# A fused attention and feed-forward kernel: the first two token blocks with eight plain products in place of Strassen's seven, all elementwise sums on VectorE, and six staging buffers for the weights

## The chip, the cores and the metric

One core of a Trainium2 chip runs the kernel. The metric is device time in microseconds (us) of one execution; lower is better. The kernel before took 928.1 us, the median of three runs (927.41 to 931.62). The engines are TensorE (PE, with PEld for its weight loads), VectorE (DVE), ScalarE (ACT), GpSimd (POOL) and SyncE (SP, which here only issues DMAs). An engine works through its own instructions in order, and waits where one of them needs something that is not there yet.

## The reference

Inputs are q, k, v of shape (8 batches, 8 heads, 576 positions, 64) in float32, and w_in (512 x 2048) and w_out (2048 x 512), which arrive in float64.

```python
q_s = softmax(q, axis=-1)            # over the 64 features
k_s = softmax(k, axis=2)             # over the 576 positions
kv  = einsum('bhsd,bhse->bhde', k_s, v)
x   = einsum('bhsd,bhde->bhse', q_s, kv)   # then as 4608 tokens x 512
h   = x @ w_in
out = (h * sigmoid(1.702 * h)) @ w_out     # 4608 x 512
```

## The kernel before, in words

The 4608 tokens are nine blocks of 512. For a block, eight steps run; a step takes one pair of 128-wide column groups of w_in (group p and group p + 8), computes h for them (FFN1), applies the GELU, and adds the product with the matching 256 rows of w_out into four PSUM banks (FFN2). Odd blocks take the pairs backwards. Each float32 operand of these matmuls is held as a high part and a low part, and a product is three matmuls: high by high, high by low, low by high.

FFN1 uses Strassen's scheme in Winograd's form: w_in's pair (512 x 256) and the block's x (512 x 512) are taken as 2 x 2 quarters, and seven products of quarters (`ffn1`, line 714) replace eight. A product is six matmuls of 256 columns. Sums of quarters of x are made per block (`x_sums`, line 664, split into high and low at lines 681 and 684); sums of quarters of the weights are made once, in block 0, when a pair is first converted (`conv_wi`, lines 332 and 338). After a product, ACT copies a bank (line 738) and DVE adds banks together (line 727).

The float64 weights are converted to float32 by bit operations on their words: ACT takes the high word (`high`, line 288), DVE shifts and merges the low word (`low`, line 297, and `narrow`, line 293), ACT rounds the result to its high part, and a subtraction gives the low part (line 338 for w_in, 384 for w_out). The raw words of a pair's w_in and later of its w_out lie in the same tile (tags `wo{p}0` and `wo{p}1`), so w_out can only be loaded after w_in was merged. Converted w_in tiles `wa` and `wb` are a ring of two pairs; each pair is stored to DRAM in block 0 (line 341, on SP) and fetched again in later blocks by DMAs that GpSimd issues (line 360). w_out stays in SBUF.

Attention for the next block runs in between: maxima of k over positions (`k_max`), subtraction and exponential (`k_sub`), the k-by-v product (`kv_pairs`, line 562), softmax of q (`q_soft`), transposes, and the product that gives x (`x_pairs`, line 638). For batches 0 and 1 the maximum over partitions is made with a transpose on TensorE (lines 502 to 510), later with GpSimd's `partition_all_reduce` (line 488).

What sets the order: the function adds every operation to a `Plan` with an engine, a cost, what it reads and writes, and a rank. `due` gives each a due time, counted back from TensorE's operations in order of rank; `forward` then walks through time and lets each free engine take the ready operation that is due first. What comes out is the order in which each engine gets its instructions. Operations marked `EITHER` may go to DVE or POOL, whichever is free first; in blocks 0 and 1 these are the sums, subtractions and low parts. The plan books 0.5 us on SP for a DMA.

Of the kernel before, what the change touches and what calls it, by code (L numbers as in the profile page):

```python
# [18 lines left out]
class Plan:  # L19
# [7 lines left out]

# [3 lines left out]
    EITHER = ("DVE", "POOL")  # L31
# [22 lines left out]
    def due(self):  # L54
        ops = self.ops
        at = [float("inf")] * len(ops)
        time = 0.0
        for n in sorted((n for n, o in enumerate(ops) if o[0] == "PE"), key=lambda n: (ops[n][3], n)):
            at[n] = time
            time += ops[n][1]  # L60
        for n in reversed(range(len(ops))):
            for d in ops[n][2]:
                e, cost, _, _, _, _, size = ops[d]
                cost = cost[0] if e is self.EITHER else cost
                need = cost + self.HOP + (size / self.RATE + self.LAND if size else 0.0)
                at[d] = min(at[d], at[n] - need)
        return at

    def forward(self, due):
# [3 lines left out]
        ready = {e: [] for e in (*free, self.EITHER)}  # L73
# [5 lines left out]
        wire, table = 0.0, {"POOL": "sum"}  # L79
        began, start, end = [], [0.0] * len(ops), 0.0  # L80
        self.taken = {}
        now = 0.0
        while len(began) < len(ops):
# [3 lines left out]
            for e in free:  # L87
                mine = [ready[e]] + ([ready[self.EITHER]] if e in self.EITHER else [])
                mine = [r for r in mine if r]
                if free[e] > now or not mine:  # L90
                    continue
                _, n = heapq.heappop(min(mine))
                kind, cost, _, _, _, needs, size = ops[n]
                if kind is self.EITHER:
                    self.taken[n] = e
                    cost, needs = (cost[0], None) if e == "DVE" else (cost[1], needs)
# [17 lines left out]
            times = [f for e, f in free.items() if f > now and (ready[e] or e in self.EITHER and ready[self.EITHER])]  # L114
# [14 lines left out]
    def emit(self):  # L129
        for n in self.order():  # L130
            run = self.ops[n][4]
            if n in self.taken:
                run(self.taken[n])
            else:
                run()


def dve(n):
    return 0.16 + n / 920
# [4 lines left out]


def pool(n):
    return 0.25 + n / 440
# [3 lines left out]
def efficient_attention_then_gelu_ffn(  # L151
# [8 lines left out]
):  # L160

# [45 lines left out]
    engines = {"DVE": nc.vector, "POOL": nc.gpsimd}  # L207
    summed = []

    def sums():  # L210

        summed.append(("sums", len(summed)))
        return summed[-1]

    def sb_op(shared, n, reads, writes, rank, run):

        if shared:
            plan.add(
                plan.EITHER, (dve(n), pool(n)), reads, (*writes, sums()), rank, lambda e: run(engines[e]), table="sum"
            )  # L220
        else:
            plan.add("DVE", dve(n), reads, writes, rank, lambda: run(nc.vector))

    ident = sb("ident", [P, P])
    kvn = [sb(f"kvn{i}", [P, NP, D]) for i in range(2)]
    xa = sb("xa", [P, 2, 2, HT])
    xb = sb("xb", [P, 2, 2, HT])
    s1, s2, s4 = (sb(f"s{i}", [P, 2, HT]) for i in (1, 2, 4))
    xs = [[sb(f"x{s}{o}", [P, 2, HT], F32R) for s in "hl"] for o in range(7)]
    gt = [[sb(f"g{i}{u}", [P, 2, HT]) for i in range(2 - u)] for u in range(2)]  # L230
    gs = [[[sb(f"g{s}{i}{u}", [P, 2, HT], F32R) for u in range(2)] for i in range(2)] for s in "hl"]
    ta, ts, tu = (sb(f"t{s}", [P, HT]) for s in "asu")
# [7 lines left out]
    cols = [sb(f"col{i}", [P, 1]) for i in range(2)]  # L240
# [3 lines left out]
    wa = [sb(f"wa{i}", [P, 2, 3, 2 * P], F32R) for i in range(2)]  # L244
    wb = [sb(f"wb{i}", [P, 2, 4, 2 * P], F32R) for i in range(2)]
    kept = [
        (dram.tile([P, 2 * 3 * 2 * P], F32, name=f"ka{p}"), dram.tile([P, 2 * 4 * 2 * P], F32, name=f"kb{p}"))
        for p in range(NS)
    ]

    make_identity(nc, ident)
# [5 lines left out]
    plan.add("POOL", 0.7, (), ("ident",), -3000, lambda: None)  # L257
# [8 lines left out]
    def load_w(p, kind, rank):  # L266
        for jj in range(2):
# [11 lines left out]

            held = [("st", 1, jj, m) for m in range(3 + jj)] if p == SPARE and kind == "wi" else []  # L280
            plan.add("SP", plan.ISSUE, (), (tag, *held), rank + 0.01 * jj, run, size=2 * DM * 4 * P)
# [19 lines left out]

    stages = [None, None]
    SPARE = NS - 1

    def stage(p):
        n = p % 2 if p < SPARE else 0
        if stages[n] is None:
            stages[n] = [  # L310
                sb(f"st{n}{i}", [P, 3 + i, 2 * P], tag=f"wo{SPARE}{i}" if n else None) for i in range(2)
            ]
        return stages[n], [[("st", n, i, m) for m in range(3 + i)] for i in range(2)]

    def conv_wi(p, rank):
        i = p % 2
        (sa, sb_), (KA, KB) = stage(p)
        for jj, (s, K) in enumerate(((sa[:, 0:2], KA[0:2]), (sb_[:, 2:4], KB[2:4]))):
            T = f"wo{p}{jj}"
            f = flat(s)  # L320
# [3 lines left out]

            plan.add("ACT", 0.67, (T,), K, rank, lambda f=f, w=w: high(f, w()))
            plan.add("DVE", 0.40, (T,), (T,), rank, lambda w=w: low(w()))
            plan.add("DVE", 0.69, (T, *K), K, rank, lambda f=f, w=w: narrow(f, w()))
        B11, B21, T2, T1, T4, T3, B22 = [(sa[:, m], KA[m]) for m in range(3)] + [(sb_[:, m], KB[m]) for m in range(4)]
        for (o, ok), (x, xk), (y, yk) in ((T1, T3, B11), (T2, B22, T1), (T4, B21, T2), (T3, B22, T3)):

            def run(E, o=o, x=x, y=y):
                E.tensor_tensor(out=o, in0=x, in1=y, op=ALU.subtract)  # L332

            sb_op(True, 2 * P, (xk, yk), (ok,), rank, run)
        for u, tl, f, K, n in (("wa", wa[i], sa, KA, 3), ("wb", wb[i], sb_, KB, 4)):

            def run_l(E, tl=tl, f=f):
                E.tensor_tensor(out=tl[:, 1], in0=f, in1=tl[:, 0].bitcast(F32), op=ALU.subtract)  # L338

            def run_s(tl=tl, u=u):  # L340
                nc.sync.dma_start(out=kept[p][u == "wb"], in_=tl.bitcast(F32).rearrange("p s n f -> p (s n f)"))

            plan.add("ACT", act(n * 2 * P), K, ((u, i),), rank, lambda tl=tl, f=f: nc.scalar.copy(tl[:, 0], f))
            sb_op(True, n * 2 * P, (*K, (u, i)), ((u, i),), rank, run_l)
            plan.add("SP", plan.ISSUE, ((u, i),), ((u, "kept", p),), rank, run_s, size=n * 4 * P * P * 4)
# [6 lines left out]
    def load_kept(t, step):  # L352
# [4 lines left out]
        for u, tl, n, off in (("wa", wa[i], 3, 5), ("wb", wb[i], 4, 13)):  # L357

            def run(u=u, tl=tl):
                nc.gpsimd.dma_start(out=tl.rearrange("p s n f -> p (s n f)"), in_=kept[p][u == "wb"])  # L360

            plan.add("POOL", 1.0, ((u, "kept", p),), ((u, i),), R(t, step - 2, off), run, size=n * 4 * P * P * 4)

    nt = [0]

    def next_tmp():
        nt[0] += 1
        return nt[0] % 2

    def conv_wo(p, rank):  # L370
        for jj in range(2):
            i = next_tmp()
# [389 lines left out]
    def ffn2(t, step):  # L762
# [3 lines left out]
        for c in (2, 3, 0, 1):  # L766
# [15 lines left out]
            if step < NS - 1:  # L782
                continue
# [90 lines left out]
```

## Time and profile before

| what | value |
|---|---|
| median of three runs | 928.1 us |
| the profiled execution | 929.58 us |
| its span, first to last instruction | 927.7 us |
| mean granted TensorE clock | 0.971 |
| PE busy | 865.3 us (93%) |
| DVE busy | 557.3 us (60%) |
| ACT busy | 492.8 us (53%) |
| POOL busy | 180.7 us (19%) |

All times of single instructions and stretches come from this one execution. Of its 929.58 us, 1.9 us lie outside the span. An engine is busy from an instruction's start to its end, so an instruction that is held up while it runs counts as busy too. Where instructions of one engine follow each other closely, they overlap a little; what one costs is then the distance between two starts.

### The profile page before, as it was taken

Reading aid. Unit: us, or ns where it says so; the run is one execution under the profiler, and the core shown is the slowest. Engines: PE = TensorE matmul, PEld = TensorE weight load, DVE = VectorE, ACT = ScalarE, POOL = GpSimd, SP = SyncE. Lnnn points to the kernel's source line nnn. Section 1 sums busy time; section 2 is a strip of 40 time slices with the busy share of each in tenths; the row PEclk is TensorE's granted clock in tenths of the full one; section 3 lists DMA queues with packets and bytes.
Section 4 is the critical chain, followed back from the end, with each engine's and each line's share of the span. In section 5 each row is a group of like instructions: output and inputs, shape, how many; then the busy total and the mean of one; then the engine's idle time right before and its main releaser. Section 6 shows DMA issues by size and latency. Waiting matters only on the chain.

```text
span 927.7 us, 15134 instructions
## 1 busy us (share of the span) xinstructions
PE 865.3 (93%) x5896; PEld 750.5 (81%) x5896; DVE 557.3 (60%) x1080; ACT 492.8 (53%) x867; POOL 180.7 (19%) x204
## 2 busy tenths in 40 slices
PE   3678777899999999999999899999999999999998
PEld 2466656788888789889888798888988988898896
DVE  6899998977653558763535387644436643353333
ACT  3657765676853397863433777633347543343222
POOL 4665565732001201000002010010000000000100
PEclk9889877999999999999999999999999999999999
DMA  9956975359516866455167664542455255416541
GB/s 286 279 190 232 295 216 203 113 204 253 161 42 205 232 189 171 159 174 167 46 195 227 172 191 141 177 159 81 157 176 169 67 159 165 153 46 205 165 153 46
DMA packets 115272, 158.29 MB, mean 171 GB/s; under 512 B 75776, under 2 KB 94208, under 8 KB 108032
## 3 DMA queue, kind: packets, MB, share of 16 engines
q0 software_dynamic: 13824, 88.09, 29.6%
q1 hardware_dynamic: 101376, 69.22, 25.4%
q8 instruction: 47, 0.77, 0.3%
q14 instruction: 25, 0.20, 0.1%
HBM read 133.17 MB, written 24.12 MB: 170 GB/s over the span
## 4 chain that ended last, share of the span: by engine, by line
PE 76%; DVE 14%; DMA 4%; SPq 2%; issue 2%; ACT 2%; DVEq 0%; POOL 0%
PE bank L776 37%; PE bank L714 33%; PE bank L562 3%; DMA kt<-in_k 2%; PE bank L638 2%; PE bank L617 1%; DVE tmp L293 1%; DVE mx L483 1%; DVE raw L297 1%; DVE m L482 1%; DVE g L727 1%; DMA qt<-in_q 1%; DVE xl L684 1%; DVE st L332 1%; DVE w L384 1%
## 5 line engine op out<-in xcount | busy, mean ns | idle before, releaser
L776 PE MATMUL bank<-w,gh 128*128 128x512 f32 x1152 | 371.0, 403 | 3.8 <-DVE w L384 3.2
L714 PE MATMUL bank<-xh,wb 128*128 128x256 f32 x1152 | 254.4, 285 | 8.1 <-DVE ts L727 3.7
L776 PE MATMUL bank<-w,gl 128*128 128x512 f32 x576 | 231.0, 401 | 2.4 <-DVE gl L758 1.4
L714 PEld LDWEIGHTS bank<-xh,wb 128*128 128x128 f32 x1152 | 199.0, 192 | 24.3 <-DVE ts L727 4.6
L776 PEld LDWEIGHTS bank<-w,gh 128*128 128x128 f32 x1152 | 190.8, 191 | 25.2 <-DVE w L384 4.4
L714 PE MATMUL bank<-xh,wa 128*128 128x256 f32 x864 | 187.5, 291 | 15.3 <-DVE wa L338 6.6
L714 PEld LDWEIGHTS bank<-xh,wa 128*128 128x128 f32 x864 | 148.2, 195 | 28.8 <-DVE wa L338 7.4
L730 ACT ACTIVATE g<-g 128x512 f32<-128x512 f32 (+1 forms) x144 | 75.6, 525 | 171.3 <-DVE g L727 167.3
L714 PE MATMUL bank<-xl,wb 128*128 128x256 f32 x576 | 164.1, 285 | 0.3 <-DVE xl L684 0.3
L776 PEld LDWEIGHTS bank<-w,gl 128*128 128x128 f32 x576 | 109.8, 191 | 30.8 <-DVE gl L758 3.2
L714 PE MATMUL bank<-xl,wa 128*128 128x256 f32 x432 | 124.5, 288 | 2.0 <-POOL xl L684 2.0
L714 PEld LDWEIGHTS bank<-xl,wb 128*128 128x128 f32 x576 | 109.5, 190 | 11.8 <-DVE xl L684 0.5
L758 DVE TENSOR_TENSOR gl<-g,gh 128x512 fp32r<-128x512 f32 x136 | 93.5, 693 | 22.8 <-ACT gh L755 22.3
L727 DVE TENSOR_TENSOR tu<-bank,ta 128x256 f32<-128x256 f32 x72 | 30.3, 421 | 107.0 <-PE bank L714 106.8
L755 ACT CAST gh<-g 128x512 fp32r<-128x512 f32 x144 | 89.4, 621 | 4.3
L714 PEld LDWEIGHTS bank<-xl,wa 128*128 128x128 f32 x432 | 84.0, 195 | 7.7 <-POOL xl L684 2.3
L360 POOL DMA_DIRECT2D wa<-ka x48 | 25.9, 539 | 329.0 <-PE bank L714 329.0
L360 POOL DMA_DIRECT2D wb<-kb x48 | 25.5, 531 | 252.3 <-PE bank L714 250.9
L730 ACT ACTIVATE g<-bank 128x256 f32<-128x256 f32 x72 | 27.7, 385 | 78.7 <-PE bank L714 77.5
L738 ACT COPY ta<-bank 128x256 f32<-128x256 f32 x72 | 26.8, 372 | 59.8 <-PE bank L714 59.3
L727 DVE TENSOR_TENSOR g<-bank,ts 128x256 f32<-128x256 f32 x72 | 30.3, 421 | 40.6 <-PE bank L714 40.2
L727 DVE TENSOR_TENSOR g<-bank,tu 128x256 f32<-128x256 f32 x72 | 30.4, 422 | 37.1 <-PE bank L714 36.4
(103 smaller groups left out, 988.7 us busy)
## 6 DMA issues: line engine op xcount, KB each, us to landing
wb<-kb POOLq DMA_DIRECT2D x48, 1024.0 KB, 5.4
wa<-ka POOLq DMA_DIRECT2D x48, 768.0 KB, 4.8
out<-tmp SPq DMA_DIRECT2D x36, 256.0 KB, 3.1
kt<-in_k SPq DMA_DIRECT2D x32, 256.0 KB, 3.7
raw<-in_moe_w_in SPq DMA_DIRECT2D x16, 512.0 KB, 6.7
raw<-in_moe_w_out SPq DMA_DIRECT2D x16, 512.0 KB, 4.0
kb<-wb SPq DMA_DIRECT2D x8, 1024.0 KB, 5.2
vt<-in_v SPq DMA_DIRECT2D x56, 128.0 KB, 5.2
```

The source lines that it names most:

```text
L293: nc.vector.scalar_tensor_tensor(fi, fi, 3, w[:, :, 0], ALU.logical_shift_left, ALU.bitwise_or)
L297: nc.vector.tensor_scalar(lo, lo, 29, None, ALU.logical_shift_right)
L360: nc.gpsimd.dma_start(out=tl.rearrange("p s n f -> p (s n f)"), in_=kept[p][u == "wb"])
L562: nc.tensor.matmul(pk[r0 : r0 + D, m, cols], lhs, rhs, start=c == 0, stop=c == CM, tile_position=(0, r0))
L638: nc.tensor.matmul(po[ro], kvn[b % 2][ri, hp, :], qx[ri], start=True, stop=True, tile_position=((a ^ odd) * D, a * D),)
L714: nc.tensor.matmul(ph[bk], tl[:, s, place, c * P : (c + 1) * P], x[:, c, :], start=opens and c == 0 and e == 0, stop=c == 1 and e == 2, sk ...
L727: return lambda: nc.vector.tensor_tensor(out=o, in0=ph[bk], in1=x, op=ALU.add)
L730: return lambda: nc.scalar.activation(o, x, AF.Gelu_apprx_sigmoid)
L738: vec("ACT", act(n), (ZB,), (A,), 2, lambda: nc.scalar.copy(a, ph[Z]))
L755: vec("ACT", act(2 * n), half, (H,), slot, lambda c=c, gh=gh: nc.scalar.copy(gh, c))
L758: E.tensor_tensor(out=gl, in0=c, in1=gh.bitcast(F32), op=ALU.subtract)
L776: nc.tensor.matmul(bank[c], l, r, start=first_ and e == 0, stop=last and e == 2)
```

## The change

Blocks 0 and 1 compute FFN1 with eight plain products per step: two column groups times four quarters of 128 rows, each three matmuls of 512 columns (`plain1`). Block 0 therefore needs only w_in itself in high and low parts (`wj`), and `conv` converts w_in and w_out in the same way; staging uses two `tmp` tiles and four `wide` ones. Block 0 stores w_in's parts to DRAM; block 1 fetches them, and `sums` makes Strassen's four sums of w_in (`wt`) from them on DVE and stores those too. From block 2 on a step fetches three pieces in place of two, of 1 MB, 0.5 MB and 0.25 MB. Nothing is marked `EITHER` any more. The maximum over partitions is made by `partition_all_reduce` for all batches, and the identity matrix is built after batch 0's maxima.

```diff
-    EITHER = ("DVE", "POOL")
...
+    def conv(p, kind, rank):
+        for jj in range(2):
+            ff, T = next_tmp(6)
...
+            plan.add("ACT", 0.66, (K,), (T,), rank, lambda ff=ff, w=w: high(ff, w()))
+            plan.add("DVE", 0.38, (K,), (K,), rank, lambda w=w: low(w()))
+            plan.add("DVE", 0.69, (K, T), (T,), rank, lambda ff=ff, w=w: narrow(ff, w()))
+            plan.add("ACT", 0.62, (T,), (KD,), rank, c5)
+            plan.add("DVE", 0.69, (KD, T), (KD,), rank, c6)
...
+    def plain1(t, step):
+        i, gi = pair(t, step) % 2, step % 2
+        for jj, bk in enumerate((Y, Z)):
...
+                for e, (l, r) in enumerate(((0, 0), (0, 1), (1, 0))):
+                    nc.tensor.matmul(
+                        bank[bk], w[:, l, c, :], x[:, r], start=c == 0 and e == 0, stop=c == KC - 1 and e == 2
+                    )
...
-        if b > 1:
-            plan.add("POOL", 0.92, (M, *summed), (M,), rank, reduce, table="max")
-            return
+        plan.add("POOL", 0.92, (M,), (M,), rank, reduce, table="max")
...
-        sb_op(t < 2, e, (K, M), (K,), rank, run_b)
+        plan.add("DVE", 2 * dve(e), (K,), (K, M), rank, run_m)
...
-            at(R(t, p), lambda rank, t=t, p=p: ffn1(t, p))
+            at(R(t, step), lambda rank, t=t, step=step: (plain1 if t < 2 else ffn1)(t, step))
```

On SP, the kernel before has these rows between the sixth load of w_in and the first stores of converted tiles (`kt`, `vt`, `kl`, `vl` and `qt` are attention's tiles of batch 1, `ka` the DRAM copy):

```order
L273 DMA raw<-in_moe_w_in 128x4x256 x6
L448 DMA vt_113<-in_v 128x4x64 x2
L448 DMA vt_114<-in_v 128x4x64 x2
L448 DMA vt_115<-in_v 128x4x64 x2
L417 DMA kt_109<-in_k 128x2x256
L417 DMA kt_110<-in_k 128x2x256
L278 DMA raw<-in_moe_w_out 128x1024
L407 DMA kl<-in_k 64x8x64
L417 DMA kt_111<-in_k 128x2x256
L417 DMA kt_112<-in_k 128x2x256
L448 DMA vt_116<-in_v 128x4x64 x2
L278 DMA raw<-in_moe_w_out 128x1024 x3
```

The changed kernel has there, from the third of its four pairs of `vt` loads on (`kept` is the DRAM copy):

```order
L449 DMA vt_90<-in_v 128x4x64 x2
L449 DMA vt_91<-in_v 128x4x64 x2
L469 DMA qt_92<-in_q 16x8x64
L469 DMA qt_92<-in_q 112x8x64
L408 DMA kl<-in_k 64x8x64
L418 DMA kt_86<-in_k 128x2x256
L418 DMA kt_87<-in_k 128x2x256
L411 DMA vl<-in_v 64x8x64
L265 DMA raw<-in_moe_w_in 128x4x256
L469 DMA qt_93<-in_q 16x4x64 x2
L469 DMA qt_93<-in_q 112x4x64 x2
L270 DMA raw<-in_moe_w_out 128x1024 x3
```

The last loads of `vt`, the first loads of q for block 1, the last row of v and a seventh load of w_in have moved ahead of the first load of w_out.

On DVE, the conversion of the second pair of w_in in the kernel before has these rows (`st10` and `st11` stage the pair, `wa0` holds high and low parts of the first pair):

```order
L293 SCALAR_TENSOR_TENSOR st10_173<-st10_173,raw_221 128x512
L332 TENSOR_TENSOR st01_172<-st01_172 128x256
L293 SCALAR_TENSOR_TENSOR st11_174<-st11_174,raw_229 128x512
L332 TENSOR_TENSOR st11_174<-st11_174,st10_173 128x256
L332 TENSOR_TENSOR st10_173<-st11_174 128x256
L338 TENSOR_TENSOR wa0_136<-st00_171,wa0_136 128x768
```

The changed kernel has these around the end of the second pair's conversion (`wj11` is the second column group of the second pair, staged in `tmp0`; `raw_392`, `raw_396`, `w_483`, `w_502`: w_out of the first pair; `gl0`: low part of the GELU's result):

```order
L720 TENSOR_TENSOR gl0_79<-g00_74,gh0_77 128x512
L288 TENSOR_SCALAR raw_392<-raw_392 128x512
L284 SCALAR_TENSOR_TENSOR wide_113<-wide_113,raw_392 128x512
L319 TENSOR_TENSOR wj11_112<-tmp0_82,wj11_112 128x512
L288 TENSOR_SCALAR raw_396<-raw_396 128x512
L284 SCALAR_TENSOR_TENSOR wide_113<-wide_113,raw_396 128x512
L319 TENSOR_TENSOR w_483<-wide_113,w_483 128x512
```

The sums of quarters have left block 0, every subtraction for a low part stands on DVE, and the one for `wj11` stands behind the first work on w_out.

## Rows read from the trace of the kernel before

**Rows 1.** Busy time of each engine in four stretches of the span (from the start to 45 us, to 186, to 275.4, to the end); then the granted TensorE clock, the busy share of the DMA engines and their rate in GB/s.

```profile
0.00:45.00 45.00, 22.61 (x210) 16.49 (x210) 34.26 (x64) 21.19 (x43) 24.23 (x27) 0.92 0.95 279
45.00:186.00 141.00, 112.45 (x659) 91.18 (x660) 131.95 (x196) 91.74 (x155) 83.55 (x58) 0.86 0.64 210
186.00:275.40 89.40, 89.30 (x638) 77.94 (x637) 61.92 (x136) 63.23 (x108) 14.66 (x21) 1.00 0.56 171
275.40:927.70 652.30, 640.97 (x4393) 564.88 (x4391) 329.16 (x686) 316.65 (x563) 58.25 (x100) 0.99 0.51 155
```

**Rows 2.** ACT's instructions in order of time (start, duration): the copy of a bank that each step makes after its second product, of block 0's first two steps and of the first step of blocks 1 and 2.

```profile
41.51 0.36 ACT L738 COPY ta<-bank 128x256 f32<-128x256 f32 x1
61.23 0.37 ACT L738 COPY ta<-bank 128x256 f32<-128x256 f32 x1 [0.57 <-PE bank L714]
...
187.41 0.35 ACT L738 COPY ta<-bank 128x256 f32<-128x256 f32 x1
276.86 0.37 ACT L738 COPY ta<-bank 128x256 f32<-128x256 f32 x1 [0.92 <-PE bank L714]
```

**Rows 3.** Instructions in order of time: the same maximum on DVE twice, and the instruction that POOL runs beside the second of them.

```profile
14.41 0.29 DVE L483 TENSOR_TENSOR mx<-m 128x128 f32<-128x128 f32 x1
...
53.18 2.32 DVE L483 TENSOR_TENSOR mx<-m 128x128 f32<-128x128 f32 x1
...
52.83 2.53 POOL L338 TENSOR_TENSOR wb<-st,wb 128x1024 fp32r<-128x1024 f32 x1
```

**Rows 4.** Groups of DVE's instructions by form (count, busy us, mean ns of one): two rows of the stretch from 0 to 186 us, then the same two forms from 190 to 927 us.

```profile
L483 DVE TENSOR_TENSOR mx<-m 128x128 f32<-128x128 f32 x12 | 10.2, 853 | 0.4
L482 DVE TENSOR_TENSOR m<-kt 128x256 f32<-128x256 f32 x12 | 10.2, 852 | 1.4 <-DMA kt<-in_k 1.4
...
L482 DVE TENSOR_TENSOR m<-kt 128x256 f32<-128x256 f32 x20 | 8.6, 430 | 6.6 <-DMA kt<-in_k 6.6
L483 DVE TENSOR_TENSOR mx<-m 128x128 f32<-128x128 f32 x20 | 6.1, 304 | 0.7
```

**Rows 5.** DVE's instructions in order of time, where several follow without a gap: low parts of 512 columns, then a merge of 512, a shift of 512 and the next start.

```profile
45.40 0.67 DVE L684 TENSOR_TENSOR xl<-xb,xh 128x512 fp32r<-128x512 f32 x1
46.00 0.68 DVE L684 TENSOR_TENSOR xl<-s,xh 128x512 fp32r<-128x512 f32 x1
...
57.35 0.68 DVE L293 SCALAR_TENSOR_TENSOR tmp<-tmp,raw 128x512 int32<-128x512 int32 x1
57.95 0.42 DVE L297 TENSOR_SCALAR raw<-raw 128x512 uint32<-128x512 uint32 x1
58.29 0.28 DVE L502 TENSOR_REDUCE col<-bank 128x1 f32<-128x128 f32 x1
```

**Rows 6.** The chain that ended last, in order of time (start, us): a batch's k-by-v product, and in block 3 FFN2 units (three matmuls of 512 columns each) and Strassen products (six of 256).

```profile
206.88 2.48 PE bank L562 x80
...
430.10 1.40 PE bank L776 x6
431.50 1.42 PE bank L714 x12
...
440.68 1.40 PE bank L776 x6
```

**Rows 7.** The start: POOL's first instruction after a fetch of its code, the k-by-v products of batch 0 and TensorE's product of x (chain, start and us), and TensorE's second product of block 0.

```profile
8.62 0.28 POOL masks.py:199 TENSOR_SCALAR_AFFINE_SELECT ident<-ident 128x128 f32<-128x128 f32 x1 [7.69 <-DMA earlywo<-in_q]
...
21.33 8.66 PE bank L562 x155
...
45.66 0.56 PE L714 MATMUL bank<-xh,wa 128*128 128x256 f32 x1
```

**Rows 8.** GpSimd's reductions over partitions (count, busy us, mean ns).

```profile
L488 POOL PARTITION_ALL_REDUCE mx<-mx x24 | 20.9, 877 | 55.9 <-DVE mx L484 49.9 <-PE bank L714 5.9
```

**Rows 9.** SP's issues in order of time (start, us until the next could follow, count).

```profile
9.90 6.89 SPq L273 DMA_DIRECT2D raw<-in_moe_w_in  x6
16.83 7.91 SPq L448 DMA_DIRECT2D vt<-in_v  x6
30.73 1.13 SPq L417 DMA_DIRECT2D kt<-in_k  x2
31.91 1.23 SPq L448 DMA_DIRECT2D vt<-in_v  x2
...
44.47 2.10 SPq L468 DMA_DIRECT2D qt<-in_q  x2
...
51.59 3.16 SPq L468 DMA_DIRECT2D qt<-in_q  x4
```

**Rows 10.** DMA issues by line (count, KB each, median us from issue to landing).

```profile
kt<-in_k SPq DMA_DIRECT2D x32, 256.0 KB, 3.7
raw<-in_moe_w_in SPq DMA_DIRECT2D x16, 512.0 KB, 6.7
raw<-in_moe_w_out SPq DMA_DIRECT2D x16, 512.0 KB, 4.0
vt<-in_v SPq DMA_DIRECT2D x56, 128.0 KB, 5.2
```

**Rows 11.** The stretch of ten microseconds with the highest rate of the DMA engines (columns as in rows 1).

```profile
90.00:100.00 10.00, 7.15 (x55) 5.41 (x51) 9.76 (x14) 8.35 (x16) 5.94 (x4) 1.00 1.07 346
```

**Rows 12.** The fetches of kept weights that GpSimd issues: time from issue to landing (min, median, max).

```profile
DMA to landing us min/median/max: 4.3/5.2/8.4
```

More of the change, by code (lines that the diff above doesn't have):

```diff
@@ L87, in forward @@
             for e in free:
-                mine = [ready[e]] + ([ready[self.EITHER]] if e in self.EITHER else [])
-                mine = [r for r in mine if r]
-                if free[e] > now or not mine:
+                if free[e] > now or not ready[e]:
                     continue
[L92 to L96, printed above, removed]
+                _, n = heapq.heappop(ready[e])
+                _, cost, _, _, _, needs, size = ops[n]
                 if needs is not None and needs != table.get(e):
@@ L113, in forward @@
                         heapq.heappush(coming, (at[u], u))
-            times = [f for e, f in free.items() if f > now and (ready[e] or e in self.EITHER and ready[self.EITHER])]
+            times = [f for e, f in free.items() if f > now and ready[e]]
             if coming:
@@ L205, in sb @@
         return const.tile(shape, dtype, name=name, tag=tag or name)
[L207 to L222, printed above, removed]
     ident = sb("ident", [P, P])
     kvn = [sb(f"kvn{i}", [P, NP, D]) for i in range(2)]
[L226 to L229, printed above, removed]
     gt = [[sb(f"g{i}{u}", [P, 2, HT]) for i in range(2 - u)] for u in range(2)]
-    gs = [[[sb(f"g{s}{i}{u}", [P, 2, HT], F32R) for u in range(2)] for i in range(2)] for s in "hl"]
-    ta, ts, tu = (sb(f"t{s}", [P, HT]) for s in "asu")
+    gs = [[sb(f"g{s}{i}", [P, 2, 2, HT], F32R) for i in range(2)] for s in "hl"]
+    tt = sb("tt", [P, 4, HT])
     tmp = [sb(f"tmp{i}", [P, DM]) for i in range(2)]
@@ L256, in efficient_attention_then_gelu_ffn @@
         nc.vector.memset(t[:, :, :, D:W], 1.0)
-    plan.add("POOL", 0.7, (), ("ident",), -3000, lambda: None)
+    plan.add("POOL", 0.7, (), ("first",), -3000, lambda: None, table="max")
     def R(t, step, off=0.0):
@@ L278, in run @@
                     nc.sync.dma_start(out=raw, in_=w_out[j * P : (j + 1) * P, :])
-            held = [("st", 1, jj, m) for m in range(3 + jj)] if p == SPARE and kind == "wi" else []
-            plan.add("SP", plan.ISSUE, (), (tag, *held), rank + 0.01 * jj, run, size=2 * DM * 4 * P)
+            plan.add("SP", plan.ISSUE, (), (tag,), rank + 0.01 * jj, run, size=2 * DM * 4 * P)
     def words(raw):
@@ L300, in flat @@
         return x.rearrange("p n f -> p (n f)")
[L304 to L320, printed above, removed]
+    nt = {2: 0, 6: 0}
@@ L327, in conv_wi, with dst @@
[L327 to L345, printed above, removed]
+            def dst(jj=jj):
+                return wo[p, jj] if kind == "wo" else wj[p % 2][jj].rearrange("p s c f -> p s (c f)")
@@ L827, in attend @@
         at(n(5.2), x_pairs, t, 1)
-        at(n(5.5), x_sums, t)
+        if t > 1:
+            at(n(5.5), x_sums, t)
+    at(
+        -998.2,
+        lambda rank: plan.add(
+            "POOL", 0.7, tuple(("mx", i) for i in range(NP)), ("ident",), rank, lambda: make_identity(nc, ident), table="std"
+        ),
+    )
     for t in range(NB):
```

338 lines of the change are left out of this document (199 added, 139 removed).

## The prediction

> **What bounds the kernel now.** I read the stretches first, then the step marks, then what fills the engine that waits for nothing. From 186 us on TensorE is the bound: it is busy 89.3 of 89.4 us in block 1 and 641.0 of 652.3 us after it [rows 1]. Its rate there is that of the chain in block 3: two FFN2 units take 1.40 us and two products 1.42 us, and the same place comes back after 440.68 - 430.10 = 10.58 us, which is eight units and seven products at 0.70 and 0.71 [rows 6]. The start and block 0 are different: between 45 and 186 us TensorE is busy 112.5 of 141 us at a mean granted clock of 0.86 of 2.4 GHz, while DVE is busy 131.9 us, the most of all engines [rows 1]. The step marks say what that costs: block 0's first mark stands at 41.5 and block 1's at 187.4 us, 18.2 us per step where TensorE needs 10.6; block 1 then takes 276.9 - 187.4 = 89.5 us [rows 2]. So some 60 us of the span are block 0 waiting for DVE.
>
> Much of what DVE is busy with is no work of its own. A maximum over 128 columns takes 0.29 us at 14.4 us and 2.32 us at 53.2 us, and beside the long one POOL runs a subtraction of 2.53 us that ends with it [rows 3]. Over groups: in the first 186 us the two forms of the maximum take 853 and 852 ns, later, where POOL has no sums, 304 and 430 [rows 4], 24 instructions stretched by 0.55 and 0.42 us, 11.6 us in all. I read this as DVE being held up by POOL's reads of the same memory. How much DVE's own work would be follows below from spacings.
>
> **The change, part by part.** *TensorE.* A step of blocks 0 and 1 gets eight groups of three 512-column matmuls in place of seven of six 256-column ones. The nearest row is FFN2's unit, also three matmuls of 512: 0.70 us [rows 6]. So 8 x 0.70 - 7 x 0.71 = +0.63 us per step, +10.1 us over 16 steps. This is certain, and where TensorE is the bound it is paid in full.
>
> *DVE in block 0.* Spacings from [rows 5]: 46.00 - 45.40 = 0.60 for two inputs of 512 columns, 57.95 - 57.35 = 0.60 for the merge, 58.29 - 57.95 = 0.34 for the shift. A pair now needs four tiles (two of w_in, two of w_out) of shift, merge and subtraction: 4 x 1.54 = 6.2 us, 49 us for eight pairs. The low parts of the GELU's result are 16 x 0.60 = 9.6 us, those of x for two blocks 8 x 0.60 = 4.8. Attention per batch: maxima 4 x 0.78, subtractions 4 x 0.80, q 4 x 2.75 (four passes of 0.60 and small ones), 17.3 us, twice, and about 7 us of the third batch's. Sum 105 us from the start to the last pair, 11 of them before the kv products. Measured busy time is 34.3 + 131.9 = 166 us up to 186 [rows 1]. So with POOL's sums moved onto it, DVE has some 60 us less to do, if the stretch goes with them. Bounds: all of it goes (105 us), or none, since it might have another cause (then about 105 + 55 us); I take the first, because long instructions stand beside POOL's and the same forms are short wherever POOL is free.
>
> *The start.* GpSimd's code fetch ends at 8.6 us as before [rows 7]; after it come a trial reduction and four of batch 0's at 0.88 us [rows 8], done by 13 us. DVE's maxima are done by about 11.5 us, so subtraction and exponential let the kv products start near 14.5 in place of 21.3; they take 8.7 us [rows 7], x follows, and no sums of x or of weights stand between x and the first product. I put that product at 28 us; before, the second product starts at 45.66 [rows 7].
>
> *The first w_out.* On SP, w_out's first load now stands behind more of batch 1's loads. From the end of the six w_in loads at 16.8 us [rows 9]: eight vt at 0.62 to 1.32 us each, 5.0 to 10.5; four kt and two tails about 3.3; qt0 2.1, qt1 3.2, one w_in 0.5 [rows 9]. So the issue falls between 31 and 37 us, and the data 4.0 us later [rows 10]; with the queue full I take 41. DVE meets w_out's shift before the subtraction for wj11, which the last four products of step 1 need. TensorE has 12 products of 0.70 from 28 us, to 36.5, and then waits until about 43: 6 us. Lower end 0, when w_out lands at 35.
>
> *The rest of block 0.* Until block 1's first product TensorE has 8 x 5.6 us of FFN1, seven steps of FFN2 at 5.6 us, and attention for batch 1 of about 6 us (2.5 for kv [rows 6], transposes and x the rest): 90 us. From 28 us with the 6 us wait that is 124. After w_out's arrival DVE has some 75 us left, to 118 us, so it runs just ahead of TensorE; the chains ACT, DVE, ACT, DVE of each conversion then cost some waits. I add 1 us a step, and 2 us for matmuls at the lower clock after waits. That is 134 us, against 187.4 - 1.4 = 186.0 before: 52 us gained.
>
> *DMA.* Loads and stores up to there: q, k, v of three batches 10.2 MB, w_in and w_out in float64 16.8, w_in's parts 8.4; 35.4 MB. At the best ten microseconds of the trace, 346 GB/s [rows 11], 102 us; at 279, the first 45 us [rows 1], 127 us. Both end before 134, the second only just.
>
> *Block 1.* Eight steps at 11.2 us and attention: 89.5 + 8 x 0.63 = 94.5 us. DVE gets the weight sums, 2 x 0.60 + 4 x 0.34 + 1.14 = 3.7 us a step; it was busy 61.9 of 89.4 us [rows 1], so there is room, and no product of block 1 reads them. ACT's table swaps sit in GELU's path; 2 us for that and the passage to block 2, whose x parts wait for the last plain products. 96.5 us, a loss of 7.
>
> *Blocks 2 to 8.* TensorE's work is the same. A weight tile is now held until a step's slot 10 of 15, 7 us into it, and needed two steps, 21 us, after that step's start. The slowest fetch landed after 8.4 us [rows 12]; 14 us are there. Nothing.
>
> Sum: 929.6 - 52 + 7 = 884.6 us for an execution like the profiled one, which is 1.5 us above the median of the runs; I say 884.
>
> **A rule weighed.** Attention's v and q come in pieces of 256 bytes. A vt load of 128 KB lands after 5.2 us, a kt load of 256 KB after 3.7 [rows 10]: half the bytes in more time. The Trainium skill ("DMA: Bandwidth & Descriptors", Specifications) says that a transfer needs pieces of at least 512 bytes to run at line rate; the rows agree in kind. Two batches of such pieces are 4.2 MB here. At half rate they would count double, and by the rule 39.6 MB at 279 GB/s would take 142 us, which would put the first rival below 15 us later still.
>
> **The rivals.** *The DMA queue paces block 0.* SP issues in order, and behind stores that wait for a conversion. For it: the DMA engines' share is 0.95 in the first 45 us [rows 1], and all that follows is pulled together into two thirds of the time. Against it: 0.64 between 45 and 186 us, with 346 GB/s in places. At 279 GB/s the last w_out lands at 127 + 5 us, is converted 3 us later, and eight units (5.6 us) and the rest of the step follow: block 1 begins at about 146, 12 us later than forecast: 897.
>
> *Block 0 runs without waits.* If w_out lands at 35 us and DVE keeps ahead, block 1 begins at 28 + 90 + 2 = 120 us: 870. Against it: in-order engines that hand a tile to and fro.
>
> *Blocks 2 to 8 pay.* Three fetches per step stand in GpSimd's queue, between its 24 reductions, whose waits for DVE come to 49.9 us [rows 8]. If a fetch comes late at each of seven batches by 3 us, 905. The 14 us of slack speak against it.
>
> *Slower: the stretch stays.* If DVE's long instructions have another cause than POOL, DVE has 160 us of work up to the last pair, a step of block 0 stays at 18 us, and block 1 begins at 186 or later: 929.6 + 7 = 937. It decides from the point where block 1 begins after 179 us. [rows 3, 4] speak against it.
>
> **How the numbers follow.** Forecast 0.55 (its own range 876 to 893), DMA pace 0.18, no waits 0.12, later blocks 0.06, stretch stays 0.04, and 0.05 for places between 905 and 925. 0.5%, 4.6 us, is about what a measurement here can tell from no change. Faster: all but the last two and a piece, 0.94; same 0.02; slower 0.04. The range from 870 to 902 leaves out the slow cases and a part of the smooth one.
>
> **What would show it.** Right: DVE's maxima at 0.3 and 0.43 us in the first 100 us; the first plain product near 28 us; one wait of TensorE of some 6 us before wj11's products; block 1's first product near 134 and block 2's near 230; steps of 11.2 us and more in block 1, 10.58 later. Wrong: DVE's instructions still long with POOL silent; a step of block 0 over 14 us; DMA landings above 10 us in block 0; waits of TensorE for `wt` after block 1.

## The result, and the profile after

The changed kernel takes 876.35 us, the median of four runs (875.62 to 879.44); the kernel before took 929.01 us beside it. The ratio is 0.944, 95% interval 0.940 to 0.947. The forecast was 884, with a range from 870 to 902. The profiled execution, the slowest of the four, took 879.44 us, 50.1 less than the one before.

Four stretches of it, columns as in [rows 1]: to the first product of the FFN, to block 1's first, to block 2's first, to the end.

```profile
0.00:30.50 30.50, 14.66 (x184) 12.22 (x185) 24.61 (x63) 12.80 (x26) 5.14 (x11) 1.00 0.97 268
30.50:126.40 95.90, 93.57 (x498) 72.22 (x497) 88.38 (x176) 76.12 (x129) 7.89 (x8) 1.00 0.90 285
126.40:222.20 95.80, 95.80 (x513) 76.70 (x512) 82.64 (x158) 76.97 (x107) 15.99 (x17) 1.00 0.64 201
222.20:877.60 655.40, 641.97 (x4393) 564.73 (x4391) 333.47 (x686) 328.12 (x573) 90.46 (x142) 0.99 0.52 154
```

TensorE is now busy 93.6 of 95.9 us in block 0, at full granted clock, where [rows 1] show 112.5 of 141 at 0.86. Block 0 ends 59.6 us earlier (186.0 to 126.4), block 1 is 6.5 longer (89.3 to 95.8), and the rest 3.0 longer in this execution (655.4 us). The other traces of changed kernels below take 646.3 to 652.8 us for the same rest, so these 3.0 us look like this execution's own and not like the change's.

TensorE's instructions (start, us): the first product, the two places where a step's last product and the next step's first two stand together, and block 2's first product. The second row that says x9 holds block 1's first product, at 126.4.

```profile
30.52 1.63 PE L702 MATMUL bank<-xp,wj 128*128 128x512 f32 x3
...
114.65 2.23 PE L702 MATMUL bank<-xp,wj 128*128 128x512 f32 x9
...
125.75 2.23 PE L702 MATMUL bank<-xp,wj 128*128 128x512 f32 x9
...
222.21 0.85 PE L749 MATMUL bank<-xo,wt 128*128 128x256 f32 x6
```

What TensorE waited for between 28 and 240 us (us, times, longest) is one line:

```profile
PE bank L702 <- ACT wj L316: 2.0, 1, 2.0
```

VectorE's maxima and shift from 0 to 128 us (count, busy, mean ns), which answer to [rows 4]:

```profile
L288 DVE TENSOR_SCALAR raw<-raw 128x512 uint32<-128x512 uint32 x32 | 13.5, 422 | 1.4 <-DMA raw<-in_moe_w_out 1.3
L483 DVE TENSOR_TENSOR m<-kt 128x256 f32<-128x256 f32 x12 | 5.2, 430 | 1.6 <-DMA kt<-in_k 1.6
L484 DVE TENSOR_TENSOR mx<-m 128x128 f32<-128x128 f32 x12 | 3.9, 326 | 0.4
```

So 852 and 853 ns have become 430 and 326.

### The profile page after: what moved, and what is told of

Read it like the earlier page. It is cut to its first block, busy times and chain, and to the rows that moved or that the text cites. A ratio compares the mean times of both kernels' runs of the same rounds, so it can differ in the third digit from the quotient of the medians.

```text
span 877.6 us, 14492 instructions
## 1 busy us (share of the span) xinstructions
PE 846.0 (96%) x5584; PEld 725.9 (83%) x5584; DVE 529.1 (60%) x1081; ACT 494.0 (56%) x833; POOL 119.5 (14%) x177
## 3 DMA queue, kind: packets, MB, share of 16 engines
q0 software_dynamic: 25248, 83.37, 30.5%
## 4 chain that ended last, share of the span: by engine, by line
PE 81%; DMA 9%; SPq 3%; DVE 3%; ACT 3%; issue 1%; DVEq 0%; ACTq 0%
PE bank L812 40%; PE bank L749 29%; PE bank L702 7%; DMA qt<-in_q 3%; DMA kt<-in_k 2%; PE bank L612 2%; PE bank L542 2%; PE bank L591 1%; SPq L449 1%; DMA raw<-in_moe_w_in 1%; DMA kept<-wj 1%; SPq L469 1%; DMA vl<-in_v 1%; DMA vt<-in_v 1%; DMA raw<-in_moe_w_out 1%
## 5 line engine op out<-in xcount | busy, mean ns | idle before, releaser
L749 PEld LDWEIGHTS bank<-xo,wt 128*128 128x128 f32 x1344 | 188.6, 190 | 28.8 <-DVE tt L762 10.1
L749 PE MATMUL bank<-xo,wt 128*128 128x256 f32 x1344 | 196.4, 284 | 9.0 <-DVE tt L762 8.4
L749 PEld LDWEIGHTS bank<-xo,wj 128*128 128x128 f32 x1008 | 137.7, 189 | 12.7 <-DVE g L762 1.9
L749 PE MATMUL bank<-xo,wj 128*128 128x256 f32 x1008 | 147.5, 282 | 0.3 <-DVE g L762 0.3
L762 DVE TENSOR_TENSOR g<-bank,tt 128x256 f32<-128x256 f32 x168 | 70.9, 424 | 108.5 <-PE bank L749 107.3
L765 ACT ACTIVATE g<-g 128x512 f32<-128x512 f32 x112 | 58.8, 525 | 137.6 <-DVE g L762 134.0
L762 DVE TENSOR_TENSOR tt<-bank,tt 128x256 f32<-128x256 f32 x112 | 47.3, 422 | 122.6 <-PE bank L749 84.3
L348 POOL DMA_DIRECT2D wj<-kept x96 | 59.4, 619 | 403.0 <-PE bank L749 346.8
L702 PE MATMUL bank<-xp,wj 128*128 128x512 f32 x384 | 104.5, 398 | 2.2 <-ACT wj L316 2.0
L702 PEld LDWEIGHTS bank<-xp,wj 128*128 128x128 f32 x384 | 71.6, 189 | 20.9 <-ACT wj L316 3.3
```

The source lines that it names most:

```text
L348: "POOL", 1.0, (key,), (ring,), R(t, step - 2, off), lambda: nc.gpsimd.dma_start(out=out(), in_=src), size=size
L702: nc.tensor.matmul(bank[bk], w[:, l, c, :], x[:, r], start=c == 0 and e == 0, stop=c == KC - 1 and e == 2)
L749: nc.tensor.matmul(ph[bk], w, x[:, r, c, :], start=opens and c == 0 and e == 0, stop=c == 1 and e == 2, skip_group_check=True,)
L762: return lambda: nc.vector.tensor_tensor(out=o, in0=ph[bk], in1=x, op=ALU.add)
L765: return lambda: nc.scalar.activation(o, x, AF.Gelu_apprx_sigmoid)
```

## The experiments

Each kernel ran beside the kernel before. Ratios are to that kernel; differences are to the changed kernel's 876.35 us. The kernel before had medians of 929.40 to 929.46 us beside them, against 929.01 beside the changed kernel. Except in w_out_early and w_out_early2, the planner orders all engines anew after an edit, so an experiment also has a new order.

### GpSimd's sums

**sums_on_dve**, in the kernel before:

```diff
-        if shared:
+        if False:
             plan.add(
```

> The kernel before with every sum that its planner could give to GpSimd put on VectorE instead; Strassen's products, the transposes for the maxima and the two staging buffers stay. Theory (GpSimd's sums held VectorE up about as much as they relieved it): VectorE's instructions return to the durations of the later blocks (128x256 maxima 0.43 us, shift of raw words 0.42, merge 0.69), which makes some 113 us of its own, and the 78 sums come back at about 0.63 us each, 49 us; block 0 ends within 10 us of where it ended (186), time 915 to 938 us. Rival (the 166 us that VectorE was busy were work, and the sums on GpSimd a relief): 49 us more on the bound engine, time about 975 us.

Measured: 909.58 us, ratio 0.978 (0.975 to 0.981). VectorE's groups from 22 to 160 us:

```profile
L297 DVE TENSOR_SCALAR raw<-raw 128x512 uint32<-128x512 uint32 x32 | 12.8, 419 | 0.0
L482 DVE TENSOR_TENSOR m<-kt 128x256 f32<-128x256 f32 x4 | 1.6, 409 | 0.0
L483 DVE TENSOR_TENSOR mx<-m 128x128 f32<-128x128 f32 x4 | 1.2, 292 | 0.1
```

The stretch up to block 1's first mark, columns as in [rows 1]:

```profile
37.50:160.00 122.50, 105.31 (x651) 86.62 (x652) 112.69 (x236) 85.73 (x152) 0.00 (x0) 0.90 0.76 259
```

With 78 sums more to do, VectorE is done earlier, and is still the busiest engine of block 0. The rival falls. The theory was too modest: VectorE's busy time up to block 1 is 139 us, not 113 + 49 = 162. Block 1's first mark comes at 160.0 in place of 187.4 [rows 2]; block 2's at 257.7 in place of 276.9:

```profile
160.01 0.37 ACT L738 COPY ta<-bank 128x256 f32<-128x256 f32 x1
...
257.66 0.37 ACT L738 COPY ta<-bank 128x256 f32<-128x256 f32 x1 [0.94 <-PE bank L714]
```

The 8 us between are in block 1, which now holds the k-by-v products of two batches.

**low_on_pool**, in the changed kernel:

```diff
+            on_pool = p >= 3 and (jj or kind == "wo")
...
-            plan.add("DVE", 0.69, (KD, T), (KD,), rank, c6)
+            if on_pool:
+                plan.add("POOL", 1.41, (KD, T, *RED), (KD, sums_key()), rank, c6, table="sum")
+            else:
+                plan.add("DVE", 0.69, (KD, T), (KD,), rank, c6)
```

`RED` and `sums_key` keep GpSimd's subtractions behind its reductions for batch 1 and ahead of those for batch 2; the same holds in idle_sums and idle_copies.

> The changed kernel with three of the four low parts of each of the pairs 3 to 7 made on GpSimd, 15 subtractions of 128x512 that VectorE no longer makes. Theory (a sum on GpSimd costs VectorE about as much in longer instructions as it takes off it): VectorE gives off 15 x 0.69 = 10 us and pays about half of 15 x 1.65 = 25 us, so nothing is won, and each low part comes 1 us later for TensorE: 876 to 884 us, with VectorE's 0.69 us instructions at 0.80 us or more. Rival (sums on GpSimd relieve VectorE): 872 to 876 us, no TensorE wait in block 0.

Measured: 889.22 us, ratio 0.957 (0.952 to 0.961), 12.9 us slower. VectorE's groups between 45 and 128 us:

```profile
L733 DVE TENSOR_TENSOR gl<-g,gh 128x512 fp32r<-128x512 f32 x12 | 9.4, 787 | 0.0
L494 DVE TENSOR_TENSOR m<-kt 128x256 f32<-128x256 f32 x5 | 4.3, 856 | 0.0
```

TensorE's two longest waits between 28 and 250 us:

```profile
PE bank L825 <- DVE gl L733: 5.5, 5, 2.3
PE bank L715 <- ACT wj L322: 4.2, 1, 4.2
```

Ten microseconds of work taken off VectorE made the kernel slower than either theory said: TensorE, which in the changed kernel waits for VectorE nowhere in block 0, now waits for its low parts of the GELU's result (L733). Not all of the 12.9 us is GpSimd's: the wait of 4.2 us ends at 43.6 us, before the first moved subtraction at 72.7, and the place in TensorE's order that stood at 51.15 us already stands at 52.74. These 1.6 us come of the new order.

**idle_sums**, in the changed kernel:

```diff
+                    nc.gpsimd.tensor_tensor(out=o, in0=x[:, 0], in1=x[:, 1], op=ALU.add)
+                for _ in range(3):
+                    plan.add("POOL", 1.41, (KD, *RED), (("tt", 2 * jj), ("tt", 2 * jj + 1), sums_key()), rank, run_x, table="sum")
```

> The changed kernel with 30 more sums on GpSimd in block 0, six for each of the pairs 3 to 7 behind its conversion: they read wj and write a tile that nothing uses before block 1, so no engine waits for a result of theirs. Theory (GpSimd's sums lengthen VectorE's two-input instructions that run beside them): 30 sums of 1.6 to 1.76 us, as the rows of before have them, are some 50 us; before, 109 us of such sums lengthened VectorE's work by about 56 us, so here by about 25 us; VectorE has some 8 us to spare in block 0, so the time rises by 8 to 20 us to 884 to 897, and the 0.69 us instructions show a mean of 0.85 us or more between 45 and 128 us. Rival (the sums on GpSimd are free for the others, and what lengthened VectorE before was its own waits): 875 to 879 us, and 0.69 us as now.

Measured: 906.78 us, ratio 0.976 (0.972 to 0.980), 30.4 us slower; the four runs go from 900.91 (the profiled one) to 909.13. VectorE's instructions in order of time, and GpSimd's three sums that run beside them from 67.76 to 72.47:

```profile
67.76 4.71 POOL L337 TENSOR_TENSOR tt<-wj 128x512 f32<-128x512 f32 x3 [15.27 <-DVE wj L325]
...
66.38 0.69 DVE L595 TENSOR_TENSOR qt<-qt,qm 128x512 f32<-128x512 f32 x1
...
68.19 1.79 DVE L737 TENSOR_TENSOR gl<-g,gh 128x512 fp32r<-128x512 f32 x1
69.90 0.67 DVE L592 TENSOR_REDUCE qm<-qt 128x8 f32<-128x512 f32 x1
70.61 0.55 DVE L593 TENSOR_SCALAR qm<-qm 128x8 f32<-128x8 f32 x1
71.19 0.20 DVE L594 RECIPROCAL qm<-qm 128x8 f32<-128x8 f32 x1
71.43 1.60 DVE L595 TENSOR_TENSOR qt<-qt,qm 128x512 f32<-128x512 f32 x1
```

The same instruction takes 0.69 us at 66.38 and 1.60 at 71.43. TensorE's two longest waits between 28 and 280 us, both for VectorE, and ScalarE's wait for GpSimd:

```profile
PE bank L829 <- DVE w L325: 6.2, 4, 4.0
PE bank L719 <- DVE wj L325: 6.0, 5, 3.2
...
ACT wj L322 <- POOL tt L337: 5.8, 3, 2.2
```

Nobody waits for what the sums write, but they read `wj`, a ring of two pairs, and so ScalarE's rounding of a later pair had to wait for them three times, first from 120.9 us on. Until then TensorE had fallen back from 1.2 us behind the changed kernel (at 67.7 us, with 397 matmuls done) to 14.7 us (at 120.9 us, with 593). These 13.5 us fell beside the sums with no engine waiting for GpSimd; in the rest of the 30.4 us VectorE's longer instructions and ScalarE's waits are not parted. The mechanism of the theory holds for the first part. Its size (8 to 20 us) is too small for the whole, and this path through the ring it did not have.

**idle_copies**: the same with `nc.gpsimd.tensor_copy(o, x[:, 0])`.

> As idle_sums, but each of the 30 GpSimd instructions is a copy of one 128x512 input to the same unused tile, so it reads one operand where a sum reads two. It parts two readings of idle_sums (906.8 us, VectorE's shift of raw words 0.77 us in place of 0.42). Theory (any elementwise work on GpSimd holds up the VectorE instructions beside it, in proportion to the time that it runs): if a copy takes 1 to 1.5 us, 30 to 45 us of GpSimd, 890 to 906 us, and the shift again at 0.6 us or more. Rival (it is the second operand of the sums that collides): 876 to 882 us, VectorE's durations as in the changed kernel.

Measured: 885.92 us, ratio 0.954 (0.949 to 0.959), 9.6 us slower; the four runs go from 880.12 (the profiled one) to 891.24. The copies, and VectorE's shift between 45 and 128 us:

```profile
L337 POOL COPY tt<-wj 128x512 f32<-128x512 f32 x30 | 25.6, 853 | 46.6 <-ACT wj L322 45.3
L288 DVE TENSOR_SCALAR raw<-raw 128x512 uint32<-128x512 uint32 x25 | 12.2, 487 | 0.0
```

Neither side has it whole. The copies run 25.6 us, less than the 30 to 45 that I priced, and lengthen VectorE's instructions too (the shift 0.49 in place of 0.42), so it is not the second operand alone. ScalarE waits for a copy once, 1.2 us. Between its last sum or subtraction and its next reduction GpSimd stands still for 6.0 us in idle_sums and 6.3 us in low_on_pool, with nothing that the profile shows to wait for; behind the copies it does not. In all three kernels TensorE waits for none of the reductions that follow, up to 280 us.

### The staging buffers

**two_buffers**, in the changed kernel; **three_buffers** is the same with `next_tmp(3)`:

```diff
-            ff, T = next_tmp(6)
+            ff, T = next_tmp(2)
```

> The changed kernel with two staging buffers in the conversion of weights in place of six. Theory (the buffers are not what shortened block 0): one half of a pair holds its buffer for a chain of about 3.3 us (0.66 + 0.69 + 0.62 + 0.69 and the hops between engines), 32 halves through two buffers are 53 us, well under the 98 us of block 0: 876 to 882 us. Rival (the six buffers carry a good part of the gain): 886 us or more, TensorE waiting for wj or w in block 0.

Measured: 892.64 us, ratio 0.961 (0.957 to 0.965), 16.3 us slower. My theory falls. What TensorE, then SP waited for in block 0, the longest lines:

```profile
PE bank L701 <- ACT wj L315: 3.9, 3, 1.6
PE bank L701 <- DVE wj L318: 2.9, 3, 1.1
...
SPq L269 <- DVE tmp L283: 17.4, 8, 5.7
```

SP's loads of w_out (L269) need the place of w_in's raw words, which the merge (L283) sets free, and the merge needs a staging buffer. In the changed kernel SP's loads of w_out wait 2.9 us for the merge (there L284, into `tmp` or `wide`):

```profile
SPq L270 <- DVE tmp L284: 1.6, 2, 1.2
SPq L270 <- DVE wide L284: 1.3, 1, 1.3
```

> The changed kernel with three staging buffers in the conversion in place of six. In two_buffers a half holds its buffer for 5.6 to 6.5 us, not 3.3, because ScalarE and VectorE take other work between its four instructions, which with two buffers makes one half in 2.8 to 3.3 us where TensorE needs one in 98 / 32 = 3.06. Theory (that hold is the cost of two buffers): with three, one half in about 2.0 us, so the time is back at 876 to 880 us. Rival (it is the order in which loads of w_out go out, which any shortage of buffers delays, or all six are needed): 883 to 891 us.

Measured: 883.03 us, ratio 0.950 (0.946 to 0.954), 6.7 us slower: the rival, at its lower end. The loads of w_out still wait for shifts and merges (SP, 28 to 128 us):

```profile
SPq L270 <- DVE raw L288: 9.1, 4, 3.6
SPq L270 <- DVE wide L284: 4.1, 2, 2.5
SPq L270 <- DVE tmp L284: 2.9, 2, 1.7
```

That these waits of SP are the cost, rather than the chain between the engines, fits both traces but was not tried by itself.

### The place of the operands' sums

**sums_in_block0** (with two buffers) and **sums0_six** (with six, moved to other places):

```diff
-            if t == 1:
+            if t == 0:
                 at(R(t, step, 0.1), lambda rank, step=step: sums(step))
```

sums_in_block0 leaves out the fetches of pairs 0 and 1 for block 2, whose first two steps therefore multiply with the operands of pairs 6 and 7 that are still in their tiles: its time stands for the order of the work, not for the right product. sums0_six makes these fetches.

> The changed kernel with Strassen's operands of w_in made in block 0 behind each pair's conversion, no longer in block 1; with two staging buffers, since the other four lie where the operands go. Theory (block 0 is the place where VectorE is short, block 1 the one where TensorE sets the pace and VectorE has room): 8 pairs x (2 x 0.69 + 4 x 0.42 + 1.23) = 34 us more VectorE work on some 90 us in the 98 us of block 0, so block 0 ends about 26 us later, and block 1 is no shorter, since TensorE bounds it: 893 to 908 us, less whatever two_buffers differs. Rival (the move is not what counts, block 0 has room for the sums): 876 to 882 us.

Measured: 895.98 us, ratio 0.963 (0.960 to 0.966), 3.3 us above two_buffers, with intervals that overlap: the rival's side, its time too high only because two_buffers was.

> The changed kernel with Strassen's operands made in block 0 and six staging buffers, which lie here in two places that x takes only in block 2; it parts the two answers to sums_in_block0, which was only 3.3 us slower than two_buffers. Theory (with two staging buffers the chain of the conversion was the bound and hid VectorE's work; with six VectorE is): VectorE's 90 us in block 0 become 124, TensorE needs 98, so block 0 is about 20 us longer and block 1 no shorter: 890 to 905 us. Rival (the place of the sums matters little, since VectorE finds room): 876 to 882 us.

Measured: 888.91 us, ratio 0.956 (0.952 to 0.959), 12.6 us slower than the changed kernel. Time and direction are the theory's, just under its low end: of VectorE's 34 us more, 12.6 arrive in the time. Between 45 and 128 us VectorE is the busiest engine again and TensorE's granted clock 0.94:

```profile
45.00:128.00 83.00, 74.47 (x389) 56.05 (x390) 77.57 (x151) 66.24 (x107) 1.42 (x2) 0.94 0.92 303
```

### The start and the first w_out

**transposes**: `k_max` makes the maxima of batches 0 and 1 as in the kernel before (`if b > 1:` ahead of the reduction, then its four steps), and ident first.

> The changed kernel with the column maxima of batches 0 and 1 made as before: a transpose on TensorE, a maximum on VectorE, a product with ident that spreads it, a copy on ScalarE; ident is made first, and the first all-reduce goes. Theory (the reductions on GpSimd save little: in the changed kernel the four maxima of the start are spread by 13.9 us, before by about 15): the start is 1 to 3 us later, since ident waits for GpSimd's code, and some 10 us of work on VectorE and ScalarE more fits beside TensorE: 877 to 880 us. Rival (the reductions are a real part of the gain, since the start hangs on them): 884 us or more, the first plain product at 36 us or later.

Measured: 879.49 us, ratio 0.948 (0.944 to 0.953), 3.1 us slower, with intervals that overlap: the theory. Its first product stands at 31.94 in place of 30.52.

**w_out_early**: `began` is reordered after planning, so that SP issues batch 1's loads of q, of the tails and of the last two k behind w_out's first two.

```diff
+        return head + [n for n in began[: last + 1] if n in held] + began[last + 1 :]
```

> The changed kernel with the first two loads of w_out issued on SP ahead of batch 1's loads of q, of the tails and of the last two k, as soon as the raw words of w_in have left their place; the order on all other engines is the same. Theory (TensorE's 2.0 us wait before wj11's products hangs on the landing of w_out at 41.4 us, because VectorE meets w_out's shift first): w_out lands at about 36, VectorE's shift follows its instruction before it at 40.1, TensorE waits 0.7 us or less there, 874.5 to 876 us. Rival (VectorE or ScalarE is late by itself, or batch 1's loads are now the late ones): the wait stays near 2 us or moves to another place, 876 us or more.

Measured: 874.76 us, ratio 0.941 (0.938 to 0.943), not to be told from the changed kernel. VectorE meets the maximum that reads `kl`:

```profile
39.19 0.28 DVE L502 TENSOR_TENSOR mx<-mx,kl 64x128 f32<-64x128 f32 x1 [2.08 <-DMA kl<-in_k]
```

And TensorE waits:

```profile
PE bank L719 <- DVE wj L330: 2.4, 1, 2.4
```

w_out was there in time, and `kl`, put behind it, was late: the rival's mechanism. The time lies in the theory's range, but it does not part the two.

**w_out_early2** leaves `kl` and the third k ahead of w_out.

> As w_out_early, where w_out landed in time but batch 1's tail of k, put behind it, landed at 39.2 us and held VectorE up for 2.1 us instead; here the tail and the third k keep their place ahead of w_out. Theory (one late load was swapped for another): VectorE waits for neither, TensorE's wait before wj11's products falls from 2.4 to 0.7 us or less, 873 to 875 us. Rival (SP's line is simply full there, and what is put back, now the fourth k and q, is late in its turn): a wait of 1.5 us or more at another load, 874.5 to 876.5 us.

Measured: 875.14 us, ratio 0.942 (0.939 to 0.945). The wait for wj11 is 0.7 us as the theory had it; two new ones have come, which the rival had, though not from loads:

```profile
PE bank L829 <- ACT w L327: 2.1, 1, 2.1
PE bank L608 <- DVE qt L595: 1.6, 1, 1.6
PE bank L719 <- DVE wj L330: 0.7, 1, 0.7
```

**start_split**: w_out_early2, with later ranks for the second pair of tile 0's attention.

```diff
-        at(n(5.2), x_pairs, t, 1)
+        at(n(5.2), late0(x_pairs, t == 0, 1.3), t, 1)
```

> w_out_early2 with the start in another order: the second pair of the attention of tile 0 (its product of k and v, its transposes of q and its x) is put behind the first products of the FFN in TensorE's order, and the planner moves VectorE's work for it accordingly. Theory (VectorE, busy without a gap from 8.5 to 29 us, sets the first product at 30.5 us, and some of its work there is only needed later): the first product comes at about 28, and 2 to 3 us are won, 871 to 873.5 us. Rival (all of that work is needed before TensorE has 12 products in a row, so it is only paid later): 873.5 to 877 us, with new waits between 30 and 45 us as long as the gain.

Measured: 875.53 us, ratio 0.944 (0.940 to 0.947): the rival. The first product moved from 29.8 to 29.75 us only, and 2.1 us of waits for x stand behind it. No version was found that is measurably faster than the change.

## Why the prediction was right, and where it was not

**The bound and the stretch: right.** VectorE's instructions went back to 0.43 and 0.33 us, its busy time up to block 1 is 113 us (forecast 105, from distances between starts, which are shorter than busy times), and block 0 is TensorE's. But the prediction put nearly all of the gain on that, and the runs divide it: GpSimd's sums off, 19.9 us (sums_on_dve); from there to plain products, moved sums and GpSimd's reductions with two buffers, 17; from two to six buffers, 16. The 17 us in the middle were not divided further, so what the plain products alone are worth is not shown. The place of the sums is 3 us (not clear of noise) with two buffers and 13 with six, so the parts don't simply add.

**TensorE's +0.63 us per step: too much.** A step takes 125.75 - 114.65 = 11.10 us, sixteen groups of 0.694; against 10.58 that is +0.52, 8.3 us in 16 steps and not 10.1.

**The start: two errors.** GpSimd's fetch of code did not show; its reductions follow VectorE's maxima at once:

```profile
0.98 0.40 POOL L243 PARTITION_ALL_REDUCE first<-first  x1 [0.54 <-DVE first L242]
5.74 0.71 POOL L489 PARTITION_ALL_REDUCE mx<-mx  x1 [4.36 <-DVE mx L485]
```

The kv products start at 13.23 (forecast 14.5). But the first plain product comes at 30.5, not 28: VectorE is busy without a gap from 8.5 to 21.5 us with q's softmax and k's subtractions, which I had put beside the kv products at no cost; their second half starts only at 20.3.

**The first w_out: right place, wrong size.** VectorE's rows there:

```profile
41.36 0.43 DVE L288 TENSOR_SCALAR raw<-raw 128x512 uint32<-128x512 uint32 x1 [1.32 <-DMA raw<-in_moe_w_out]
42.08 0.69 DVE L284 SCALAR_TENSOR_TENSOR wide<-wide,raw 128x512 int32<-128x512 int32 x1 [0.29 <-ACT wide L279]
43.07 0.69 DVE L319 TENSOR_TENSOR wj<-tmp,wj 128x512 fp32r<-128x512 f32 x1 [0.29 <-ACT wj L316]
```

It landed at 41.4 (forecast 41), and wj11 was ready at 43.8. But the wait of TensorE ended at 43.09, before VectorE's subtraction was done. What ended it was ScalarE's rounding of wj11 to its high part, which stood behind ScalarE's own first instruction on w_out:

```profile
41.36 0.69 ACT L279 ACTIVATE wide<-raw 128x512 f32<-128x512 f32 x1 [3.12 <-DMA raw<-in_moe_w_out]
42.44 0.60 ACT L316 CAST wj<-tmp 128x512 fp32r<-128x512 f32 x1
...
43.09 2.62 PE L702 MATMUL bank<-xp,wj 128*128 128x512 f32 x9 [2.01 <-ACT wj L316]
```

So the late load is the cause that the prediction named, and the engine that passed it on is another than the one it named. The wait is 2.0 us, not 6, because TensorE, starting later and with x's product among the twelve, ended them at 41.1 and not at 36.5.

**"1 us a step" and "2 us for matmuls at the lower clock": this term failed.** No step of block 0 has such a wait, and the granted clock is 1.00. Two groups of products ran long, 1.2 us in all: three in 1.63 us at 30.52, where three take 0.85 later, and nine in 2.62 behind the wait for w_out, where nine take 2.23 (a weight load waits 0.43 us for VectorE's subtraction there). I let the chains between ScalarE and VectorE cost a wait per step without asking how far six buffers let the conversion run ahead; two_buffers shows such waits, and their size. TensorE's own work was 95.9 - 2.0 = 93.9 us, not 90, mainly because attention and the last of x take 10.0 us busy in it (L612 3.4, L591 3.1, L542 3.5) and not 6. So block 1 begins at 30.5 + 2.0 + 93.9 = 126.4, where the forecast had 28 + 6 + 90 + 10 = 134. In kind this is the rival "block 0 runs without waits", whose 120 us had the start and TensorE's work too short.

**The sum: in part luck.** Block 2 was forecast for 134 + 96.5 = 230.5 us and begins at 222.2. The errors have both signs: the start +2.5 and TensorE's own work +3.9, against the wait for w_out -4, the waits and the clock -10, and block 1 -0.7. They leave -8.3, where the last three alone would have left -14.7. The last step of the sum is off too: 884.6 less 1.5 is 883.1, and the prediction says 884.

**DMA: right, its sign wrong.** 285 GB/s in block 0, and TensorE never waits there for a transfer but through w_out above. Yet a sign came that the prediction had put down as wrong, landings above 10 us. The loads of w_in between 30 and 126 us:

```profile
DMA to landing us min/median/max: 6.1/9.0/11.0
```

No engine's wait for them reached TensorE, so this sign did not tell what it was meant to. The half rate in "A rule weighed" was my assumption; no run tries it.

**Block 1 and after.** 95.8 us (forecast 96.5). No product waits for `wt`, nor for any fetched tile after block 1, so the rival "blocks 2 to 8 pay" falls. TensorE's waits for `tt` in the later blocks are 8.4 us in the profiled execution and 5.5 in w_out_early's, where these blocks take 649.6 us in place of 655.4; why they differ was not tried. The start of block 2 leaves them out: 222.2 us in the changed kernel, 224.7 in transposes, 229.3 in three_buffers, 232.0 in idle_copies, 238.7 in sums0_six, 239.7 in low_on_pool, 241.3 in two_buffers, 252.5 in idle_sums. These distances agree with those of the medians within 0.7 us, but for sums0_six, low_on_pool and two_buffers, where they are 3 to 5 us larger.

## What to carry to other kernels

Elementwise work that GpSimd takes from a busy VectorE isn't free for VectorE: here 15 subtractions moved over made the kernel 13 us slower, and 78 moved back made it 20 us faster, each with a new order. Work whose result nobody uses still holds up whoever wants to overwrite what it reads. Count staging buffers also by what the next load waits for, and not only by the conversion's own chain; the traces fit this, and it was not tried by itself. A term such as "1 us a step" needs a row or a buffer count behind it.

## What the runs showed of the hardware that was not expected

Not all of VectorE's instructions are held up. Beside GpSimd's sums, a product of two SBUF tiles (L595) takes 1.60 us for 0.69, and TENSOR_SCALAR (L593) 0.55 for 0.17; the reduction stays at 0.67 and the reciprocal at 0.20. In the kernel before, between 22 and 160 us, an addition that reads one operand from a PSUM bank kept its time as well, while the maximum did not:

```profile
L483 DVE TENSOR_TENSOR mx<-m 128x128 f32<-128x128 f32 x8 | 8.4, 1044 | 0.3
L727 DVE TENSOR_TENSOR g<-bank,tu 128x256 f32<-128x256 f32 x6 | 2.5, 411 | 0.0
```

The Trainium skill ("SBUF — State Buffer", Who interferes with whom) says that VectorE and GpSimd share one pair of ports, which a VectorE instruction needs when it has two inputs in SBUF (against a GpSimd instruction that reads SBUF) or is a `tensor_scalar` in its two-port mode, and a `tensor_reduce` does not. The rows agree on the two inputs in SBUF, on the reduction and on the addition from PSUM, and idle_copies, whose copies read SBUF too, agrees as well. For TENSOR_SCALAR they show that it is lengthened, not in which mode it ran. The price differs: with 46 us of idle sums the kernel is 30.4 us slower, a part of it through ScalarE's waits, with 25.6 us of idle copies 9.6.
